# Attention and gated two-layer network on one core: the last tile in column halves, the first block's last products ahead of the hidden layer, and a reordered fourth visit

## The chip, the cores and the metric

The kernel runs on one core of a Trainium2 chip. The metric is the device time of one execution in microseconds, the median over executions. The profile's span runs from the first to the last instruction and is some 1.8 us shorter than the time.

## The reference

```python
# q, k, v: 8 batches x 8 heads x 1024 x 64; E, F: 64 x 1024; w_in: 512 x 2048; w_out: 2048 x 512
k_proj = einsum('ks,bhsd->bhkd', E, k)          # 1024 keys become 64
v_proj = einsum('ks,bhsd->bhkd', F, v)
attn   = softmax(q @ k_proj.T / 8)
x      = heads_side_by_side(attn @ v_proj)      # 8192 x 512
h      = x @ w_in
g      = h * clip(h + 3, 0, 6) / 6
out    = g @ w_out                              # 8192 x 512, float32
```

## The kernel before

Products are in bf16. Tokens go in blocks of 512, two per batch. TensorE does the hidden layer (16 groups of 4 products) of one block, interleaved with the output layer (tiles of 16 products) of the block before. The attention of the next batch is slipped in as four "visits" between the tiles of the output layer. The fourth visit finishes head pairs 2 and 3 and projects the keys and values of the batch after that:

```python
def scaled(self, j, av, recs):                  # VectorE: x = values * 1/sum
    for t in range(NB):
        nc.vector.tensor_mul(self.xT[:, j, t, :], av[t], recs[t])

def visit(self, n, following, later):
    ...                                         # cut: visits 0 to 2
    early = self.values(2, pmm, pmm)            # TensorE
    den, av = self.sums(3, pmm, pat), self.values(3, pat, pat)
    if following:
        following.project()                     # TensorE, 16 products
    self.scaled(2, early, self.recs)            # VectorE
    recs = self.inverses(den)                   # ScalarE: Ln, then Exp of minus
    if following:
        following.keys_out()                    # VectorE, waits for project()
        later += [following.turn] + [lambda a=a: following.values_out(a) for a in range(2)]
    return lambda: self.scaled(3, av, recs)     # VectorE, after the key copies
```

In the traces of this case each engine runs its instructions in the order in which they are emitted (e6 below only moves the key copies behind the scaling, and its records change places), so a line's place in this text is its place in its engine's queue.

The first batch is done in pieces while its inputs are still arriving. Its last products stood behind the first two products of the hidden layer:

```python
def first_block(self):
    ...                                         # cut
    busy(1)                                     # one product on ones, result unused
    products(2)                                 # values of pair 2, scaled on VectorE
    self.vals(3, nc.scalar.copy)                # projects pair 3's values, ScalarE copies them
    yield
    products(3)

def two_groups(xT, t, g, kos, more=lambda: None):
    tiles = [pmm(), pmm()]
    for i, (fo, part) in enumerate([(fo, part) for part in kos for fo in range(2)]):
        h_part(tiles[fo], xT, t, fo, part)
        if i == 0:
            more()                              # resumes first_block: products(3)
    ...
two_groups(xT, 0, g[0], ((0, 1), (2,), (3,)), lambda: next(by_pairs, None))
```

The last output tile was copied out of its one accumulator by two engines and stored through two queues:

```python
half = slice(0, d_model // 2), slice(d_model // 2, d_model)
nc.vector.tensor_copy(o_sb[:, half[0]], o_ps[:, half[0]])
nc.scalar.copy(o_sb[:, half[1]], o_ps[:, half[1]])
nc.sync.dma_start(out=o_dst[:, half[0]], in_=o_sb[:, half[0]])
nc.scalar.dma_start(out=o_dst[:, half[1]], in_=o_sb[:, half[1]])
```

The softmax here doesn't subtract the row's maximum and nothing guards it: scores larger than these inputs give would overflow.

## Time and profile before

| | before |
|---|---|
| time, median of 3 runs (range) | 510.26 us (510.22 to 510.55) |
| span of the profiled run | 508.7 us |
| TensorE busy | 98% |
| VectorE, ScalarE busy | 51%, 54% |
| TensorE waits after 25 us, except "issue" (four gaps in which one product's record is missing) | one, recorded as 0.6 us |

To see terms of some tenths of a microsecond, I cut the span at three moments. They are start times from the trace's records: the first product of the first batch's last values block (19.687 us in the kernel before), the first product of the fourth visit before batch 2 (130.517), and the first product of the last output tile (500.986). The four stretches are called start, early, middle and tail. In the kernel before they take 19.69, 110.83, 370.47 and 7.76 us.

### The profile page before, as it was taken

How to read it: one execution, taken by the hardware profiler on the slowest of the kernel's cores; microseconds unless marked ns; L12 is line 12 of the kernel's file. 1: busy time of each engine (PE TensorE's matmuls, PEld its weight loads, DVE VectorE, ACT ScalarE, POOL GpSimd, SP SyncE). 2: the span in 40 equal slices, each digit the busy share in tenths (PEclk: the TensorE clock that was granted, in tenths of full speed). 3: DMA queues.
4: the chain of work that ended last, by engine and by line, in shares of the span. 5: the costliest groups of instructions: out<-in, count | busy, mean ns of one | idle time of the engine just before them, and what ended most of it. 6: DMA issues, size and time to landing. Idle time of an engine off the chain costs nothing.

```text
span 508.7 us, 7106 instructions
## 1 busy us (share of the span) xinstructions
PE 497.5 (98%) x2750; PEld 224.3 (44%) x2802; DVE 258.0 (51%) x401; ACT 274.0 (54%) x493; POOL 37.9 (7%) x57
## 2 busy tenths in 40 slices
PE   8899999999999999999999999999999999999996
PEld 4444444444444444444444444444444444444442
DVE  3572746856755733556444743467444563334420
ACT  3657476567475545664466644674447654444431
POOL 8610020010100200002000020000000000000000
PEclk9999999999999999999999999999999999999999
DMA  9999999599299592516923188411110011101112
GB/s 170 200 205 207 199 155 239 98 170 203 53 191 203 78 220 65 125 42 105 216 63 84 52 147 175 103 51 33 43 41 34 29 43 43 43 24 39 41 51 74
DMA packets 74210, 55.39 MB, mean 109 GB/s; under 512 B 35520, under 2 KB 65984, under 8 KB 74176
## 3 DMA queue, kind: packets, MB, share of 16 engines
q0 software_dynamic: 31952, 29.36, 36.9%
q1 hardware_dynamic: 42000, 25.17, 19.2%
q10 hardware_dynamic: 224, 0.39, 0.3%
q8 instruction: 22, 0.36, 0.3%
q14 instruction: 12, 0.10, 0.1%
HBM read 59.24 MB, written 16.78 MB: 149 GB/s over the span
## 4 chain that ended last, share of the span: by engine, by line
PE 94%; DMA 2%; POOL 2%; issue 1%; DVE 0%; ACT 0%; DVEq 0%; POOLq 0%
PE mm L444 44%; PE mm L424 43%; PE at L181 3%; DMA v<-in_v_dram 2%; PE mm L227 2%; PE at L227 1%; PE at L209 1%; POOL q L97 1%; PE mm L209 1%; POOL k L101 1%; POOL v L101 0%; PE at L344 0%; DVE kp L187 0%; PE at L324 0%; PE at L312 0%
## 5 line engine op out<-in xcount | busy, mean ns | idle before, releaser
L430 DVE SCALAR_TENSOR_TENSOR g<-r,mm 128x512 bf16<-128x512 f32 x256 | 173.9, 687 | 132.3 <-ACT r L429 130.9
L444 PE MATMUL mm<-w_out_sb,g 128*128 128x512 bf16 x997 | 231.6, 379 | 1.8 <-issue 0.6
L424 PE MATMUL mm<-xT,w_in_sb 128*128 128x512 bf16 x999 | 229.1, 379 | 1.8 <-DVE xT L246 0.6
L429 ACT ACTIVATE r<-mm 128x512 f32<-128x512 f32 x256 | 152.6, 599 | 76.1 <-PE mm L424 74.2
L424 PEld LDWEIGHTS <-w_in_sb 128*128 128x128 bf16 x1024 | 99.4, 98 | 122.8 <-issue 4.8
L444 PEld LDWEIGHTS <-g 128*128 128x128 bf16 x1024 | 98.1, 98 | 121.6 <-issue 7.0
L458 ACT COPY o_sb<-mm 128x512 f32<-128x512 f32 x35 | 20.3, 587 | 91.5 <-PE mm L444 91.5
L458 DVE COPY o_sb<-mm 128x512 f32<-128x512 f32 x28 | 19.4, 692 | 67.0 <-PE mm L444 67.0
L159 ACT ACTIVATE rec<-mm 128x512 f32<-128x512 f32 x39 | 21.8, 595 | 37.0 <-PE mm L227 20.1
L163 ACT ACTIVATE rec<-rec 128x512 f32<-128x512 f32 x60 | 35.6, 638 | 0.0
L246 DVE TENSOR_TENSOR xT<-at,rec 128x512 bf16<-128x512 f32 x42 | 26.9, 680 | 5.1 <-ACT rec L163 5.1
L218 ACT ACTIVATE aT<-at 128x512 bf16<-128x512 f32 x42 | 22.1, 616 | 0.0
L199 POOL COPY mark<-kT 1x1 bf16<-1x1 bf16 x5 | 0.9, 178 | 209.0 <-DMA kT<-kp 209.0
L159 ACT ACTIVATE rec<-at 128x512 f32<-128x512 f32 x25 | 14.6, 599 | 2.3 <-PE at L344 2.3
L181 PE MATMUL at<-k,e_t 128*64 128x512 bf16 x56 | 13.4, 382 | 0.0
L181 PE MATMUL at<-v,f_t 128*64 128x512 bf16 x56 | 13.4, 382 | 0.0
L218 ACT ACTIVATE aT<-mm 128x512 bf16<-128x512 f32 x14 | 7.6, 594 | 9.5 <-PE mm L209 9.5
L187 DVE CAST kp<-at 64x512 bf16<-64x512 f32 x14 | 9.0, 678 | 4.9 <-PE at L181 4.9
L190 DVE CAST vp<-at 64x512 bf16<-64x512 f32 x14 | 9.7, 694 | 0.4
L246 DVE TENSOR_TENSOR xT<-mm,rec 128x512 bf16<-128x512 f32 x14 | 9.0, 682 | 0.6 <-PE mm L227 0.6
L84 PE MATMUL mm<-ones 128*128 128x512 bf16 x18 | 7.4, 548 | 1.5 <-DVE ones L77 1.5
L181 PEld LDWEIGHTS <-e_t 128*64 128x64 bf16 x56 | 5.6, 109 | 7.2 <-PE at L227 2.1
(62 smaller groups left out, 142.0 us busy)
## 6 DMA issues: line engine op xcount, KB each, us to landing
out_dram<-o_sb SPq DMA_DIRECT2D x63, 256.0 KB, 2.0
k<-in_k_dram POOLq DMA_DIRECT2D x7, 1024.0 KB, 15.4
v<-in_v_dram POOLq DMA_DIRECT2D x7, 1024.0 KB, 20.5
q<-in_q_dram POOLq DMA_DIRECT2D x7, 1024.0 KB, 10.5
w_out_sb<-in_moe_w_out_dram POOLq DMA_DIRECT2D x4, 512.0 KB, 16.8
k<-in_k_dram POOLq DMA_DIRECT2D x4, 256.0 KB, 5.6
v<-in_v_dram POOLq DMA_DIRECT2D x4, 256.0 KB, 7.8
w_in_sb<-in_moe_w_in_dram POOLq DMA_DIRECT2D x2, 512.0 KB, 11.7
```

The costliest lines, as they stand in the source:

```text
L159: nc.scalar.activation(ln, den, AF.Ln)
L163: nc.scalar.activation(ln, ln, AF.Exp, scale=-1.0)
L181: nc.tensor.matmul(ps[e * KP:(e + 1) * KP], ef_t[e][:, so, :], kqv[self.b]["kv"[e]][:, :, so, :], start=(so == 0), stop=(so == SO - 1))
L209: nc.tensor.matmul(tiles[r][t * KP:(t + 1) * KP, a * HT:(a + 1) * HT], self.kT[r * D:(r + 1) * D, 2 * j + a, :], qT[r * D:(r + 1) * D, j, ...
L218: nc.scalar.activation(self.aT[j][:, r].rearrange("p a n -> p (a n)"), tiles[r], AF.Exp, scale=scale)
L227: nc.tensor.matmul(tiles[t][c:c + D].rearrange("p (r n) -> p r n", r=2), stationary(r, 2 * j + a), self.aT[j][r:r + KP, :, a, :], start=Tr ...
L246: nc.vector.tensor_mul(self.xT[:, j, t, :], av[t], recs[t])
L424: nc.tensor.matmul(h_ps, w_in_sb[:, ko, fo * P:(fo + 1) * P], xT[:, ko, t, :], start=(ko == 0), stop=(ko == KO - 1))
L429: nc.scalar.activation(r, h_ps, AF.Relu, bias=0.5, scale=1.0 / 6.0)
L430: nc.vector.scalar_tensor_tensor(g[:, fo, :], r, 1.0, h_ps, op0=ALU.min, op1=ALU.mult)
L444: nc.tensor.matmul(o_ps, g[:, fo, c * P:(c + 1) * P], w_out_sb[:, fo, :], start=(fo == 0), stop=(fo == FO - 1))
L458: (copy or nc.scalar.copy)(o_sb, o_ps)
```

## The change

The intent is to shorten what TensorE waits for at three places: behind the key copies, behind the first hidden products, and behind the last tile's copies. This is the diff, its core:

```diff
@@ fourth visit
+            den = self.sums(3, pmm, pat)
             early = self.values(2, pmm, pmm)
-            den, av = self.sums(3, pmm, pat), self.values(3, pat, pat)
+            av = self.values(3, pat, pat)
+            recs = self.inverses(den)
+            self.scaled(2, early, self.recs)
             if following:
                 following.project()
-            self.scaled(2, early, self.recs)
-            recs = self.inverses(den)
-            if following:
-                following.keys_out()
                 later += [following.turn] + [lambda a=a: following.values_out(a) for a in range(2)]
-            return lambda: self.scaled(3, av, recs)
+            def rest():
+                self.scaled(3, av, recs)
+                if following:
+                    following.keys_out()
+            return rest
@@ first_block
             self.vals(3, nc.scalar.copy)
-            yield
+            busy(1)
             products(3)
@@ second_group, last tile only
+            for e, copy, dma in ((0, nc.vector.tensor_copy, nc.sync), (1, nc.scalar.copy, nc.scalar)):
+                half = slice(e * d_model // 2, (e + 1) * d_model // 2)
+                o_ps = pmm()[:, :d_model // 2]
+                for fo in range(FO):
+                    nc.tensor.matmul(o_ps, g[:, fo, c * P:(c + 1) * P], w_out_sb[:, fo, half],
+                                     start=(fo == 0), stop=(fo == FO - 1))
+                o_sb = opool.tile([P, d_model], f32, tag="o_sb", name="o_sb")[:, :d_model // 2]
+                copy(o_sb, o_ps)
+                dma.dma_start(out=o_dst[:, half], in_=o_sb)
+            return
   (cut: the two half copies and stores of before go)
@@ first groups
-    two_groups(xT, 0, g[0], ((0, 1), (2,), (3,)), lambda: next(by_pairs, None))
+    two_groups(xT, 0, g[0], ((0, 1, 2), (3,)))
```

More of the change, by code (lines that the diff above doesn't have):

```diff
@@ L441, in second_group @@
     def second_group(b, t, g, c, copy=None):
+        o_dst = out_rows(b, t, c)
+        if (b, t, c) == (B - 1, NB - 1, SB - 1):
+            for e, copy, dma in ((0, nc.vector.tensor_copy, nc.sync), (1, nc.scalar.copy, nc.scalar)):
[8 more added lines that the diff above has]
+            return
         o_ps = pmm()
@@ L448, in second_group @@
         o_sb = opool.tile([P, d_model], f32, tag="o_sb", name="o_sb")
-        o_dst = out_rows(b, t, c)
-        if (b, t, c) == (B - 1, NB - 1, SB - 1):
-            half = slice(0, d_model // 2), slice(d_model // 2, d_model)
-            nc.vector.tensor_copy(o_sb[:, half[0]], o_ps[:, half[0]])
-            nc.scalar.copy(o_sb[:, half[1]], o_ps[:, half[1]])
-            nc.sync.dma_start(out=o_dst[:, half[0]], in_=o_sb[:, half[0]])
-            nc.scalar.dma_start(out=o_dst[:, half[1]], in_=o_sb[:, half[1]])
-            return
         (copy or nc.scalar.copy)(o_sb, o_ps)
@@ L473, with two_groups @@
     first = First(xT)
-    by_pairs = first.first_block()
-    next(by_pairs)
+    first.first_block()
     x_next = x_tile()
     g = [g_tile(), g_tile()]
-    def two_groups(xT, t, g, kos, more=lambda: None):
+    def two_groups(xT, t, g, kos):
         tiles = [pmm(), pmm()]
-        for i, (fo, part) in enumerate([(fo, part) for part in kos for fo in range(2)]):
-            h_part(tiles[fo], xT, t, fo, part)
-            if i == 0:
-                more()
+        for part in kos:
+            for fo in range(2):
+                h_part(tiles[fo], xT, t, fo, part)
         for fo in range(2):
             h_out(tiles[fo], g, fo)
-    two_groups(xT, 0, g[0], ((0, 1), (2,), (3,)), lambda: next(by_pairs, None))
+    two_groups(xT, 0, g[0], ((0, 1, 2), (3,)))
     for fo in range(2, FO):
```

## The prediction

> **What bounds the kernel now.** I read three views, in this order: the page's busy table with the chain that ended last, then the list of waits of TensorE, then the records in order of time at the four places that the diff touches.
>
> The page of the kernel before (busy us, share of the span, instructions; then the 40 slices; then the chain):
>
> ```profile
> span 508.7 us, 7106 instructions
> PE 497.5 (98%) x2750; PEld 224.3 (44%) x2802; DVE 258.0 (51%) x401; ACT 274.0 (54%) x493; POOL 37.9 (7%) x57
> ...
> PE   8899999999999999999999999999999999999996
> ...
> PE 94%; DMA 2%; POOL 2%; issue 1%; DVE 0%; ACT 0%; DVEq 0%; POOLq 0%
> ```
>
> The reader is to see that TensorE is busy almost without a break, that VectorE and ScalarE are half idle, and that the chain which sets the end runs over TensorE for 94% of the span. So a change pays only if it removes TensorE idle time or TensorE instructions, or shortens the two ends: the start of some 20 us, where the first attention block waits for loads, and the tail after the last product. PE busy is not PE at its peak, so I checked the pace: in the records the 128x512 products start every 0.2158 us (15 steps from 500.986 to 504.224). Starts 0.43 us apart are one missing record.
>
> The waits of TensorE (who waited for whom, us, times, longest), all there are:
>
> ```profile
> PE mm L84 <- DVE ones L77: 1.5, 1, 1.5
> PE mm L444 <- issue: 0.6, 4, 0.2
> PE mm L344 <- ACT aT L364: 0.6, 1, 0.6
> PE mm L424 <- DVE xT L246: 0.6, 1, 0.6
> PE at L312 <- DMA v<-in_v_dram: 0.5, 1, 0.5
> PE mm L337 <- DVE kT L307: 0.3, 1, 0.3
> ```
>
> After the start there is one real wait: L424, the first products of the next batch's hidden layer, wait once for the scaled attention output xT of L246. This is all that reordering the fourth visit can win. The records in order of time around it:
>
> ```profile
> 132.82 0.38 PE L181 MATMUL at<-k,e_t 128*64 128x512 bf16 x1
> 132.83 0.38 PE L181 MATMUL at<-v,f_t 128*64 128x512 bf16 x1
> 133.14 1.47 PE L424 MATMUL mm<-xT,w_in_sb 128*128 128x512 bf16 x5
> 135.21 1.02 PE L424 MATMUL mm<-xT,w_in_sb 128*128 128x512 bf16 x4 [0.60 <-DVE xT L246]
> ...
> 133.28 1.28 DVE L187 CAST kp<-at 64x512 bf16<-64x512 f32 x2 [0.76 <-PE at L181]
> 134.48 1.27 DVE L246 TENSOR_TENSOR xT<-at,rec 128x512 bf16<-128x512 f32 x2
> ```
>
> VectorE sits 0.76 us until the key projection is done, copies the keys for 1.28 us, and only then scales. The reciprocals were ready long before: ScalarE's last two instructions for them start at 132.15 and take 1.15 us together.
>
> The tail:
>
> ```profile
> 504.70 0.43 DVE L453 COPY o_sb<-mm 128x256 f32<-128x256 f32 x1 [16.00 <-PE mm L444]
> 505.15 0.33 SPq L455 DMA_DIRECT2D out_dram<-o_sb  x1
> 505.15 0.37 ACT L454 COPY o_sb<-mm 128x256 f32<-128x256 f32 x1 [3.34 <-DVE o_sb L453]
> 505.56 0.35 ACTq L456 DMA_DIRECT2D out_dram<-o_sb  x1
> ```
>
> The two half copies of the last tile do not run side by side: ScalarE starts when VectorE is done.
>
> **What the Trainium skill says.** "TensorE: Matmul & The Clock Gate", section Back-to-back issue gap, gives N/2.4 + 2.5 ns from start to start at full clock: 215.8 ns at 512 columns. The trace agrees (215.8, granted clock 1.000). At 256 columns it gives 109.2 ns; no such full-array product is in this trace, but 128-column ones (L312) start every 57 ns with a fresh weight load each, so weight loading should not be what limits 256. "PSUM — Partial Sum Buffer", section PSUM bank collisions raise a hardware error, says that two engines may not access one bank and quadrant together, ScalarE with VectorE included, even at other columns. That fits the serial half copies above, and two accumulators in place of one lift it. "DMA: Bandwidth & Descriptors", section Anatomy of one DMA, puts about 2.0 us on a transfer as a fixed part. The last stores took 1.8 us to land for 128 KB, the full ones 2.0 for 256 KB, so a smaller store earns little and only its start time matters.
>
> **Part 1, the last tile in column halves.** It replaces 16 products of 512 columns by 32 of 256. By the skill's formula 32 x 109.2 = 3.49 us against 16 x 215.8 = 3.45: **+0.04 us** on the path. A last product of 256 columns has less left to stream than one of 512 (recorded 379 ns, less 107 = 272), so the end of the last product moves from 504.60 to about 504.64. The first half is copied and stored under the second half's products. After the end only ScalarE's copy (0.37) and its store remain: the copy can start at about 504.72 instead of 505.155, which takes **0.44 us** from the path. The landing and the closing semaphores (505.56 to 508.7) stay. Sum: **-0.40 us**.
>
> **Part 2, batch 0's last products ahead of the early groups.** This concerns TensorE's order at 20 us:
>
> ```profile
> 20.36 0.38 PE L424 MATMUL mm<-xT,w_in_sb 128*128 128x512 bf16 x1
> 20.67 0.40 PE L344 MATMUL at<-aT,vp 64*64 64x512 bf16 x2
> 21.00 1.73 PE L424 MATMUL mm<-xT,w_in_sb 128*128 128x512 bf16 x7
> ```
>
> Before, two useful products of L424 (one record missing, at about 20.14) fill the time in which ScalarE copies the last values (20.34 to 20.61). Then come the values (20.67) and four products up to 21.86. The next needs the xT that VectorE writes until 21.87, and starts at 21.929, 0.266 after the one before it: 0.05 us lost. After the change a dummy product on ones stands in the gap. The values cannot start sooner, as they need ScalarE's copy, and all 8 products of the first two groups come after 21.00. Six precede the first that needs xT, so the 0.05 goes, but two real products of 0.216 are now behind the wait instead of inside it: 0.43 - 0.05 = **+0.38 us**. TensorE has no idle time after this in which to make it up, so it moves the end. I take this part for a small loss, whatever its intent.
>
> **Part 3, the fourth visit.** It removes and adds no instruction. TensorE runs sums, values of pair 2, values of pair 3; each step of four quarter-array products takes 0.22 to 0.23 us (starts 130.517, 130.757, 130.97), so ScalarE's logarithms begin about 0.24 us earlier, and the first reciprocal is there at about 132.5. VectorE finishes pair 2 at 132.51 and scales pair 3 at once: the half needed first is done at about 133.2, the other at 133.8, and the key copies fill 133.8 to 135.1. TensorE needs it at 134.227 + 0.216 = 134.443, so 1.2 us of slack replace the wait. It started at 135.207: **-0.76 us**, once. The other fourth visits (batches 2 to 6) lie in the first half of a batch, and xT is not read for another 60 us. There TensorE goes on 0.31 us after the projection, as at every such change of array shape, with no wait before or after the change. The visit of the first attention block has no following keys and feeds products 3 us later. All of those count zero.
>
> **Sum:** -0.40 + 0.38 - 0.76 = **-0.78 us**; 510.26 - 0.78 = 509.48, so **509.5 us**, 0.15% less.
>
> **Rivals.** First, the later key copies become the new wait. They end about 0.5 us later (135.1 against 134.56), and the transposed keys land about 2.7 us after that, near 137.8. The scores of the next visit used them at 139.18 and now would at 138.4. The slack of 0.6 is thin but positive; if it is lost, part 3 gives back a few tenths and the time is about 509.9. For it: transposes share the queues with large loads. Against it: the median of seven such landings is 2.7 us. Second, narrow products are limited by the weight loads, recorded at 98 ns each: if a load does not hide under a 109 ns product, the last tile takes up to 32 x 0.2 = 6.4 us and the kernel is near 512.5. Against it: the 57 ns pace of the 128-column products with their own loads. Third, part 2 costs nothing, because its products were waiting for something else anyway: then 509.1. Against it: the 0.2158 pace from 21.00 on leaves nothing to absorb two products. Fourth, the scaled order shifts VectorE's later work so that the hidden products wait for accumulators: against it, VectorE is 51% busy and does the same work.
>
> **Range and chances.** The three runs before spread over 0.33 us, and my three terms are each good to some 0.1 us save part 2, which could be zero. So 509.0 to 510.0 should hold it 8 times in 10. Faster or slower by 2% would take 10 us, and nothing here is of that size: within 2% at 0.98.
>
> **What would show it.** At the tail: 32 products of 256 columns about 109 ns apart, one ScalarE copy after the last, its store issued about 0.45 us after the last product's end instead of 0.96. At 20 us: a product of L84's kind before the values, then eight L424 products from about 21.0 with no gap, the first hidden activation about 0.38 later than 22.34. At the visit before batch 2: the wait of L424 for L246 gone from the list, the key copies behind the scaling. The prediction is wrong if a new TensorE wait stands in that list, if the narrow products run slower than 109 ns, or if the loads of the start shift by themselves.

## More of the kernel before

All runs profiled had a mean granted TensorE clock of 0.997 to 1.000.

## The result

| | before | after |
|---|---|---|
| time, median of 6 runs (range) | 510.41 us (510.22 to 510.55) | 509.68 us (509.24 to 510.24) |
| ratio | | 0.9987 (0.9974 to 1.0) |
| start | 19.69 | 19.58 |
| early | 110.83 | 111.21 |
| middle | 370.47 | 369.71 |
| tail | 7.76 | 7.32 |
| span of the profiled run | 508.75 | 507.82 |

The ratio is the mean time of one kernel's runs over that of the other's of the same rounds, so it is not quite the ratio of the two medians. Its interval reaches 1.0, so the times alone only just show a change, and every kernel here is within 2% of the one before. The stretches, one profile per kernel, are much steadier than the time, as the experiments will show. The change is -0.76 in the middle, -0.44 in the tail and +0.38 early. The start differs by 0.11 us with nothing changed in it.

The list of TensorE's waits in the kernel after, complete (who waited for whom, us in total, times, longest):

```profile
PE mm L84 <- DVE ones L77: 1.5, 1, 1.5
PE at L140 <- ACT ef_raw L136: 0.7, 1, 0.7
PE at L301 <- DMA k<-in_k_dram: 0.5, 2, 0.3
PE mm L342 <- DVE kT L312: 0.3, 1, 0.3
PE mm L349 <- ACT aT L369: 0.3, 1, 0.3
```

All that is left lies in the first 20 us. The wait of the hidden products (L424 before, L429 after) for L246 is gone. The records in order of time at that visit show why:

```profile
132.87 1.29 DVE L246 TENSOR_TENSOR xT<-at,rec 128x512 bf16<-128x512 f32 x2
...
133.41 3.63 PE L429 MATMUL mm<-xT,w_in_sb 128*128 128x512 bf16 x16
134.07 1.27 DVE L187 CAST kp<-at 64x512 bf16<-64x512 f32 x2
```

The scaling now starts at 132.87 instead of behind the keys, and TensorE runs 16 products without a break. The key copies come last. The tail, in the same view:

```profile
500.50 3.66 PE L454 MATMUL mm<-w_out_sb,g 128*128 128x256 bf16 x32
...
502.50 0.42 DVE L457 COPY o_sb<-mm 128x256 f32<-128x256 f32 x1 [14.30 <-PE mm L454]
502.95 0.33 SPq L458 DMA_DIRECT2D out_dram<-o_sb  x1
504.24 0.37 ACT L457 COPY o_sb<-mm 128x256 f32<-128x256 f32 x1 [2.91 <-PE mm L454]
504.64 0.35 ACTq L458 DMA_DIRECT2D out_dram<-o_sb  x1
```

The 32 narrow products take 3.66 us to the end of the last; the 16 wide ones of before took 3.62 (500.986 to 504.603). VectorE's copy and its store lie under the second half. And the early groups:

```profile
20.04 0.38 PE L84 MATMUL mm<-ones 128*128 128x512 bf16 x1
20.23 0.27 ACT L320 CAST vp<-at 128x128 bf16<-128x128 f32 x1 [0.69 <-PE at L317]
...
20.55 0.40 PE L349 MATMUL at<-aT,vp 64*64 64x512 bf16 x2
...
20.89 2.55 PE L429 MATMUL mm<-xT,w_in_sb 128*128 128x512 bf16 x11
```

The dummy (L84) stands where two real products stood, the values (L349) follow ScalarE's copy as before, and all hidden products come behind them.

### The profile page after: what moved, and what is told of

It is laid out like the page before. It is cut to its first block, busy times and chain, and to the rows that moved or that the text cites. A ratio compares the mean times of both kernels' runs of the same rounds, so it can differ in the third digit from the quotient of the medians.

```text
span 507.8 us, 7202 instructions
## 1 busy us (share of the span) xinstructions
PE 500.3 (99%) x2819; PEld 226.0 (45%) x2819; DVE 258.2 (51%) x401; ACT 274.0 (54%) x493; POOL 38.0 (7%) x57
## 4 chain that ended last, share of the span: by engine, by line
PE 96%; DMA 1%; POOL 1%; ACT 0%; issue 0%; DVE 0%; ACTq 0%; POOLq 0%
PE mm L429 44%; PE mm L462 43%; PE at L181 3%; PE mm L227 2%; DMA k<-in_k_dram 1%; PE at L227 1%; PE at L209 1%; PE mm L454 1%; PE at L349 0%; PE mm L209 0%; PE at L317 0%; POOL q L97 0%; PE at L329 0%; PE mm L349 0%; POOL k L101 0%
## 5 line engine op out<-in xcount | busy, mean ns | idle before, releaser
L429 PE MATMUL mm<-xT,w_in_sb 128*128 128x512 bf16 x1024 | 230.7, 379 | 0.0
L429 PEld LDWEIGHTS <-w_in_sb 128*128 128x128 bf16 x1024 | 99.5, 98 | 122.1 <-issue 3.8
L462 PEld LDWEIGHTS <-g 128*128 128x128 bf16 x1008 | 96.6, 98 | 119.7 <-issue 7.0
L246 DVE TENSOR_TENSOR xT<-at,rec 128x512 bf16<-128x512 f32 x42 | 26.9, 683 | 4.9 <-ACT rec L163 4.3
L246 DVE TENSOR_TENSOR xT<-mm,rec 128x512 bf16<-128x512 f32 x14 | 9.0, 682 | 0.8 <-PE mm L227 0.8
L227 PE MATMUL mm<-aT,ones 64*64 64x512 bf16 x70 | 8.6, 400 | 0.0
```

What stands on the lines that cost most here:

```text
L227: nc.tensor.matmul(tiles[t][c:c + D].rearrange("p (r n) -> p r n", r=2), stationary(r, 2 * j + a), self.aT[j][r:r + KP, :, a, :], start=Tr ...
L429: nc.tensor.matmul(h_ps, w_in_sb[:, ko, fo * P:(fo + 1) * P], xT[:, ko, t, :], start=(ko == 0), stop=(ko == KO - 1))
L462: nc.tensor.matmul(o_ps, g[:, fo, c * P:(c + 1) * P], w_out_sb[:, fo, :], start=(fo == 0), stop=(fo == FO - 1))
```

## The experiments

The theory is that three independent terms add up: a wait removed at the visit before batch 2, two real products moved behind a wait in the first block, and a copy taken out of the tail. I measured it with twelve kernels, all of them correct. Each call also ran the kernel before on the same chip. The table has each kernel's median time with that of before, then the stretches of its profiled run.

| run | time / before | ratio (95%) | early | middle | tail |
|---|---|---|---|---|---|
| e1_visit_only | 509.70 / 510.46 | 0.9983 (0.9970 to 0.9997) | 110.82 | 369.71 | 7.76 |
| e2_tail_only | 510.05 / 510.46 | 0.9993 (0.9981 to 1.0006) | 111.14 | 370.46 | 7.30 |
| e3_early_only | 510.83 / 510.46 | 1.0006 (0.9994 to 1.0019) | 111.20 | 370.47 | 7.75 |
| e4_visit_tail | 509.25 / 510.46 | 0.9977 (0.9965 to 0.9990) | 110.83 | 369.71 | 7.30 |
| e5_sums_first | 510.56 / 510.46 | 1.0005 (0.9991 to 1.0020) | 111.51 | 370.47 | 7.75 |
| e6_scale_first | 509.68 / 510.46 | 0.9985 (0.9970 to 1.0000) | 110.83 | 369.71 | 7.75 |
| e7_no_dummy | 509.58 / 510.46 | 0.9982 (0.9967 to 0.9997) | 111.21 | 369.71 | 7.31 |
| e8_tail_whole | 510.02 / 510.46 | 0.9991 (0.9974 to 1.0008) | 110.83 | 370.46 | 7.24 |
| e9_unequal_tail | 509.00 / 510.57 | 0.9968 (0.9955 to 0.9980) | 110.83 | 369.71 | 6.96 |
| e10_late_weights_old_order | 510.64 / 510.57 | 0.9997 (0.9983 to 1.0011) | 112.50 | 369.71 | 7.32 |
| e11_late_weights_new_order | 510.00 / 510.57 | 0.9987 (0.9975 to 1.0000) | 111.51 | 369.71 | 7.30 |
| e12_last_store_sync | 508.97 / 510.49 | 0.9970 (0.9956 to 0.9984) | 110.83 | 369.71 | 6.99 |

The middle took one of two values, 369.71 or 370.46 to 370.47, in all fourteen profiles. This is why a difference of 0.4 us can be read from a stretch when the time's interval is over 1 us wide.

### One part at a time

The edits are the three parts of the diff above, each alone on the kernel before (e1, e2, e3), and the diff without its early part (e4).

> The kernel before with the fourth visit of the kernel after alone. Theory (one wait of TensorE for the scaled output before batch 2 is removed, nothing else): 0.76 us less; from the visit's first product to the first product of the last tile 369.7 us in the trace instead of 370.47, the other stretches unchanged, and no wait of the first hidden products for the scaled output in the list. Rival (the later key copies or the loads behind them become a new wait in the six other visits or at the next visit): the stretch shortens by less than 0.5 us and a wait for the transposed keys stands in the list.

The middle fell from 370.47 to 369.71, and the wait for L246 is gone from the list. The rival falls: the later key copies made no new wait anywhere.

> The kernel before with the last tile in two halves of columns alone. Theory (one copy instead of two behind the last product, 32 narrow products cost 0.04 us more): 0.40 us less; from the first product of the last tile to the span's end 7.3 us instead of 7.76. Rival (narrow products are bound by their weight loads at 98 ns or worse, or the lone store lands no sooner than the pair did): the stretch stays at 7.7 or grows; with exposed weight loads it grows by whole microseconds.

The tail fell by 0.46 us, to 7.30. The rival that weight loads bind the narrow products falls. There was also something not expected: the early stretch, which this edit does not touch, grew by 0.31 us. More of that below.

> The kernel before with batch 0's last products ahead of the early groups alone. Theory (two real products moved behind a wait that a dummy now fills): 0.38 us more; from the first product of the last values block (first block) to the first product of the fourth visit before batch 2, 111.21 us instead of 110.83. Rival (the products waited for something else and the move is free): 110.83 within 0.05, and the time of the kernel before.

The early stretch took 111.20 us, +0.37. The rival that the move is free falls for this run. The time is 0.37 us over before too, but its interval (0.9994 to 1.0019) can't tell that from nothing.

> The kernel after with the early part undone. Theory: the three parts add up, so this is 0.38 us less than the kernel after and 1.16 us less than the kernel before, ratio about 0.9977. Rival (the early part helps the others, or is free): within 0.1 us of the kernel after.

The stretches are those of the kernel after with the early one of the kernel before: the three terms add. The median is 509.25 us, 0.43 under the 509.68 of the kernel after. That comparison is between calls and chips; the stretches are the evidence.

### Which half of the visit's change pays

```diff
 e5: on the kernel before
-            early = self.values(2, pmm, pmm)
-            den, av = self.sums(3, pmm, pat), self.values(3, pat, pat)
+            den = self.sums(3, pmm, pat)
+            early = self.values(2, pmm, pmm)
+            av = self.values(3, pat, pat)
 e6: on the kernel before
-                following.keys_out()            # now behind scaled(3), in rest()
```

> The kernel before with only the first half of the visit's change: the sums of pair 3 are issued ahead of the values of pair 2. Theory (the order of VectorE is the whole gain, the earlier sums are slack): the logarithms start 0.24 us earlier, but scaling still stands behind the key copies, so the wait of 0.76 us stays and the stretch from the visit to the last tile stays at 370.47 us. Rival (the earlier reciprocals carry the gain): the stretch falls by 0.2 us or more.

> The kernel before with only the other half: scaling of pair 3 ahead of the key copies, sums where they were. Theory: reciprocals are ready at about 2.2 us after the visit's first product, the half that is needed first is scaled at about 2.9, TensorE wants it at 3.93, so the whole 0.76 us goes: 369.71 us from the visit to the last tile. Rival (both halves are needed): some of the wait remains, the stretch lies between 369.8 and 370.4.

The sums first alone left the middle at 370.47 and the wait in the list. The scaling ahead of the key copies alone took it to 369.71. These are e6's records of VectorE and TensorE at that visit:

```profile
132.86 1.29 DVE L246 TENSOR_TENSOR xT<-at,rec 128x512 bf16<-128x512 f32 x2 [0.30 <-ACT rec L163]
133.19 2.98 PE L429 MATMUL mm<-xT,w_in_sb 128*128 128x512 bf16 x12
...
134.07 1.27 DVE L187 CAST kp<-at 64x512 bf16<-64x512 f32 x2
```

VectorE now waits 0.30 us for the reciprocals, which are no sooner than before, and TensorE still does not wait. So the gain is all VectorE's order, and the earlier sums (0.22 us at ScalarE's first logarithm: 0.44 after the visit's first product instead of 0.66) are slack.

### What the early part costs, and what it is for

```diff
 e7: on the kernel after
             self.vals(3, nc.scalar.copy)
-            busy(1)
             products(3)
```

> The kernel after without the dummy product that it puts ahead of the last products of batch 0. Theory (the dummy lies in the wait for ScalarE's copy of the last values): nothing changes, 111.21 us from the last values block to the visit before batch 2. Rival (the dummy itself is the cost of the early part): 0.2 to 0.38 us less.

The early stretch is 111.21 us again: the dummy lies in a wait and costs nothing. The cost is the two real products that stood there.

But e2_tail_only and e5_sums_first keep the old order, and their early stretches are 111.14 and 111.51 us. In both runs the values arrived sooner (19.36 and 19.14 us, against 19.69), and TensorE shows a wait that the kernel before did not have. This is from the list of TensorE's waits of e2_tail_only:

```profile
PE mm L424 <- DVE xT L373: 0.4, 1, 0.4
```

The list names VectorE, but VectorE is not the cause. In the records of that run the first weight load of the hidden layer (LDWEIGHTS brings the weights into TensorE) waits on a transfer:

```profile
20.12 0.11 PEld L424 LDWEIGHTS <-w_in_sb 128*128 128x128 bf16 x2 [0.31 <-DMA w_in_sb<-in_moe_w_in_dram]
```

The pieces of that transfer had all landed at 20.08 us, and the load starts at 20.118. In the kernel before, the same transfer had landed at 19.93, when TensorE got there at 20.09. So in the old order the first block's last products stand behind a weight transfer, and lose when the weights land too late for the values. To test this, I made the weights late on purpose, under both orders:

```diff
 e10: on e4 (old order); e11: on the kernel after (new order)
-    for lo, n in ((0, 128), (128, 128), (256, 256), (512, 256), (768, 256),
+    for lo, n in ((256, 256), (0, 128), (128, 128), (512, 256), (768, 256),
```

> The version with visit and tail but batch 0's last products in their old place, and the first weight loads issued late on purpose: a load of 256 KB goes ahead of the two of 128 KB that the first groups need. Theory (in the old order the last products stand behind the first products of the hidden layer, and so behind the first weight load): the values of pair 3 wait until that load has landed, about 21.3 us, and the early stretch grows by a microsecond or more, to about 112.5 us.

> The kernel after with the same late weight loads. Theory: the last products run at their usual place in the records, right after the copy of the last values and before the weights, and the first groups start when the weights land, with xT ready: 0.3 to 0.6 us less than the old order under the same loads, so that the early part is a gain where the weights are late. Rival (the early part is a loss of 0.38 us in any case): 0.38 us more than the old order under the same loads.

TensorE's records in order of time, first with the old order, then with the new one:

```profile
21.49 0.61 PE L429 MATMUL mm<-xT,w_in_sb 128*128 128x512 bf16 x2 [1.50 <-DMA w_in_sb<-in_moe_w_in_dram]
22.03 0.40 PE L349 MATMUL at<-aT,vp 64*64 64x512 bf16 x2
22.36 0.39 PE L429 MATMUL mm<-xT,w_in_sb 128*128 128x512 bf16 x1
```

```profile
20.68 0.40 PE L349 MATMUL at<-aT,vp 64*64 64x512 bf16 x2
21.26 1.31 PE L429 MATMUL mm<-xT,w_in_sb 128*128 128x512 bf16 x5 [0.18 <-DMA w_in_sb<-in_moe_w_in_dram]
```

With the old order the values (L349) stand 1.5 us behind the weights. With the new order they are done before the weights land. The first group's weights had landed at 21.44 us in the one run and 21.21 in the other. From there to the visit before batch 2 it took 110.43 us (131.87 - 21.44) with the old order and 110.00 (131.21 - 21.21) with the new: 0.43 us for the new. In times it is 510.00 against 510.64. So the early part is a trade: it costs 0.38 us where the weights are there in time, and pays only where the old order would lose more than that to them. In seven of the nine old-order profiles with the usual loads (before, e1, e4, e6, e8, e9, e12; values at 19.59 to 19.91 us) the weights were in time; in e2 and e5 they were not. What the kernel after would have done with the loads of e2 and e5 was not run. An estimate: its 111.21 us, added to the starts of e2 and e5, put the visit before batch 2 at 130.58 and 130.35 us, against 130.51 and 130.65 measured there. So it would have lost 0.07 us in e2 and won 0.30 in e5.

### The tail

```diff
 e8: on the kernel before: the special case of the last tile is dropped
+        nc.scalar.copy(o_sb, o_ps)              # 512 columns
+        nc.sync.dma_start(out=o_dst, in_=o_sb)
```

> The kernel before with the last tile copied and stored whole, as every other tile: one copy of 512 columns on ScalarE and one store of 256 KB. Theory (the two half copies of before ran one after the other, 0.86 us from first start to last end, and bought nothing): the store is issued at about 0.72 us after the last product's end instead of 0.955 and lands in 2.0 instead of 1.84 us, so the tail stretch is 7.7 us, about 0.05 to 0.1 less than 7.76. Rival (halving pays even in series): the tail stretch grows by 0.2 us or more.

The direction was right and the size was missed: the tail is 7.24 us, below even the changed kernel's. Copy and store behaved as expected: the copy took 0.59 us from 504.675, and the store was waited out 2.02 us after its issue at 505.286. The other 0.43 us lie behind the landing. At the program's end SyncE works through a list of waits on semaphores, one every 0.061 us (read from the trace's raw records: no view of the profile shows them one by one). In the kernel before, the last store's semaphore is the first of eight there, at 507.413, and the eighth starts at 507.842, 0.43 us later. In e8 the last store's semaphore is the last of the list (507.306), and the waits before it ran while the store was under way. So the two half copies of before bought nothing: they ran one after the other, and one transfer more put the last store at the front of the list.

```diff
 e9: on e4
-  two halves: 256 columns VectorE + SyncE, 256 columns ScalarE + ScalarE's queue
+  384 columns VectorE + SyncE, 128 columns ScalarE + ScalarE's queue
 e12: on e9
-  384 VectorE + SyncE, 128 ScalarE + ScalarE's queue
+  384 ScalarE + ScalarE's queue, 128 VectorE + SyncE
```

> The version without the early part (visit and tail of the kernel after), with the last tile cut into 384 and 128 columns in place of two halves. Theory: the copy behind the last product falls from 0.37 to about 0.26 us (512 columns took 0.587, 256 took 0.372), the 32 products take 0.03 us more, so the tail stretch falls from 7.30 to about 7.22 us. Rival (128-column products or a store of 512-byte rows cost more than the copy saves): 7.30 us or more. The time itself can hardly show 0.08 us: about 509.2 us.

The tail fell to 6.96 us, 0.34 under the equal halves where I expected 0.08. The copy took 0.27 us instead of 0.37. The products of 128 columns kept a pace of 0.056 us, and the last one ends 3.66 us after the tile's first, as with halves. The rest, 0.23 us, is the store, which I had left out: 64 KB was waited out 1.61 us after its issue (504.248 to 505.863), where 128 KB took 1.84 (504.637 to 506.479 in the kernel after).

> The version with the visit of the kernel after, batch 0's last products in their old place and the tail of 384 and 128 columns, where now ScalarE copies and stores the first piece and VectorE copies the last one and SyncE stores it. Theory (from the records of the whole-tile run: SyncE's closing list waits for ScalarE's store first and then goes through seven more waits of 0.061 us each, but for its own last store it waits last): the seven waits run while the store is under way, 0.43 us less than the run of 384 and 128 before it, a tail stretch of 6.55 us in place of 6.96 and about 508.6 us in all. Rival (the closing list only shifts, or the order of the queues is chance): 6.9 us or more.

This was a miss: 6.99 us. The last store now went out from SyncE, but its semaphore is again the first of the eight. The records name it 107 and the first piece's 118, the reverse of e9: in these runs the numbers went to the stores in the order in which the program emits them, whichever engine issues. In e8 there is one store fewer, and its last one has number 118. My reading of e8 as SyncE's privilege was wrong. That one store more or fewer, with the unequal tail, takes the other 0.43 us was not run.

The quickest versions are e9 and e12, 509.00 and 508.97 us: the visit's change, the old early order and the unequal tail. Both beat the kernel before (510.57 and 510.49, intervals wholly under 1). The kernel after had 509.68. It was run at another time. Against it the tail's 0.33 to 0.35 us and the early 0.38 us are the evidence.

## Why the prediction was right

- **The bound.** TensorE's stream sets the end. After the start there was one wait, and every stretch moved by what was taken out of or put into that stream.
- **The visit, -0.76.** Measured -0.76, once. e6 shows that the order on VectorE does it alone, and e5 that the sums first do nothing, as the 1.2 us of slack in the prediction implied. The slack measured 1.15: the half needed first was scaled 2.77 us after the visit's first product, and TensorE took it at 3.93. The first rival, a wait for the transposed keys, did not come true: they landed 0.65 us before their use (7.26 and 7.91 us after that product), where the prediction said 0.6. Its argument that transposes share the queues with large loads does not hold: in the kernel before, the keys' transfer of 134.58 to 137.27 us moved on queue q1 alone and the loads of 10 to 18 us on q0.
- **The tail, -0.40.** Measured -0.44 to -0.46. The narrow products cost the 0.04 us predicted, at 109 ns apart. But the prediction counted this cost twice: its copy start of 504.72 already lies behind the later end of the products (504.64), so the 0.44 us to 505.155 was the whole term and no 0.04 was to be added. The second rival, exposed weight loads, falls. The prediction left out that the skill's section gives N/2.4 + 2.5 ns for an isolated product and longer or shorter times for a stream with weight loads (see the last section); here the stream followed the formula. Its aside that a smaller store earns little does not hold either: 0.23 us in e9.
- **The early part, +0.38.** Measured +0.38 in the kernel after and +0.37 in e3. The third rival, that it is free, falls for the loads of those runs. But the prediction's "a small loss, whatever its intent" was too narrow: its term took the landing times of one trace as fixed, though it named a shift of the loads among the signs of being wrong. e2 and e5 show that they are not fixed, and e10 and e11 that the sign turns with them.
- **The sum, -0.78, 509.5 us.** The three stretches give -0.82 and the medians -0.73; the measured 509.68 us lies within 509.0 to 510.0. With the 0.04 counted once the prediction's sum is -0.82, the same as the stretches. That the total came so near is partly luck: the start, which no term covers, varied from 19.14 to 20.48 us over the fourteen profiles.

## What to carry to other kernels

When one engine sets the end, go through its list of waits. Measure a wait from start to start (the list had 0.6 us where 0.76 could be won). Look for it in the queue that releases the wait: here VectorE's order was worth 0.76 us and the earlier sums on TensorE nothing. What stands first behind a transfer in an in-order queue holds back all that follows it, so judge such an order from several traces, with the landing times of each. At the end of a program, count the last store's size, and what comes behind it: the closing waits, and the place of its semaphore among them.

## What the Trainium skill lacked or had wrong

- "DMA: Bandwidth & Descriptors", Anatomy of one DMA: its fixed part of about 2.0 us is given for the path of GpSimd. The last stores from SyncE and ScalarE were waited out after 1.61 us (64 KB), 1.84 (128 KB) and 2.02 (256 KB). The growth from 64 to 256 KB, 0.41 us, is near what its rate gives (an estimate from the page: 0.45), so the fixed part here is nearer 1.5 us, by the same estimate.
- No page has the closing waits of a program one by one: SyncE took eight of them at 0.061 us each, and 0.43 us of that lay behind the last landing or under it, by the place of the last store's semaphore.
- "TensorE: Matmul & The Clock Gate", Back-to-back issue gap: N/2.4 + 2.5 ns held at 256 columns (109 measured, 109.2 by the formula) and at 128 (56 against 55.8) with a fresh 128x128 weight load per product. The section gives this formula for an isolated product. Its figures for a stream of products with their weight loads, 131 ns at 512 columns and 81 at 128, did not hold: 215.8 and 56 here.
- "TensorEngine Tiling (Array Packing)" says that a change of tiling mode drains TensorE, without a time. Here 0.31 us passed from the start of the last 512-column product to the first of the other shape, 0.09 more than the usual 0.216.
